# Sliding-window attention and token-mixing MLP on one core: k and q loaded in other pieces, the mask on VectorE, the last stores on two queues, and a new order of all work

## Chip, cores and metric

The kernel runs on one core of a Trainium2 chip. The metric is device time in microseconds, the median of repeated executions of the whole program. PE is TensorE, DVE VectorE, ACT ScalarE, POOL GpSimd and SP SyncE.

## What is computed

q, k and v are float32 of shape (8 batches, 8 heads, 576 tokens, 64). The attention has a window of 128 tokens back and a bias that falls with distance, with a slope of its own for each head; the second part mixes the tokens of each batch.

```python
rel = pos[:, None] - pos[None, :]
mask = (rel >= 0) & (rel < 128)
scores = where(mask, q @ k.T / 8 - slope[head] * abs(rel), -1e9)
x = softmax(scores) @ v                    # heads side by side: (8, 576, 512)
wq, wk = x @ w_q, x @ w_k                  # (8, 576, 64)
mixed = (wq @ wk.T / 8) @ x
out = relu(mixed) @ w_out                  # float32 (8, 576, 512)
```

## The kernel before, in words

All work is cut into some 690 named operations. `add(...)` declares each with its dependences; the text `ORDER` (lines 45 to 113) lists all of them by name with the engine that does each (P PE with the bank of PSUM, A ACT, D DVE, G POOL, S SP), and `follow` (line 140) emits them in that sequence. Every engine works through its own part of the list in order, so an operation that waits holds those behind it on its engine. A name ends in the batch and, behind the point, the part: QK4.2.0 is batch 4, key block 2, first half of the heads.

For each batch the stages are these:

- **Loads** (`Lq`, `Lk`, `Lv`, `Lt`; lines 374 to 394, issued by POOL, which converts float32 to float16). q of a batch is one load (`dma_q`) in which partition p holds rows 4p to 4p+3 of each head, so a run of 256 elements is contiguous in memory. k comes in four loads of 128 rows (`dma_k`, 64 elements to a run), v in five, and the last 64 rows of q and k of a pair of batches in `Lt`. For batch 0 six float32 loads, `LF`, are issued by SP and ACT instead, and reach the transposes `TF` and their copies `EF` without conversion. There are three buffers for k (`NNAT`), two for q (`NQ`), four for v.
- **Transposes** (`TQ`, `TK`, for batch 0 `TF` and `TJ`, tails `TT`) on PE with an identity matrix as second operand, each followed by a copy out of PSUM into `qkT` (`ETQ`, `ETK`, `EJ`, `ETT`). `TQ` (line 531) has 32 transposes of 128x64 that write column halves of PSUM, 128 columns each. `TK` (line 549) has sixteen in row halves (`tp2`, line 240): the upper and lower 64 partitions of two heads at once, 64 columns each. Both copies write dense rows.
- **Attention**: `QK` makes the scores of a key block for four heads in a pair of banks, `EXP` (ACT, line 639) exponentiates 128x1024 of them, `MUL` (DVE, line 654) multiplies both halves with a table `bias` of exp(-slope x distance), which is zero outside the window, `PV` (line 681) multiplies with v, and `RC` and `X` (DVE, lines 705 and 715) divide by the sums.
- **Mixing**, for pairs of batches: `XT`, `WK`, `WQ`, `WT`, `G`, `MX` on PE with their copies `EXT`, `EWK`, `EWQ`, `EWT`, `EG`, `RM`; then `OUT` (four matmuls of 512 columns), its copy `EO`, and the store `DO` (lines 932 to 970), all on SP. The last row group, `LAST` = (7, 3), is done in two halves, a and b.

Ahead of this stand the constants. POOL makes the identity (`ident`) and distances (`iota`, lines 303 to 305); DVE converts these (`wmc`, line 324); POOL puts a large number outside the window with four selects (`mask`, line 307); ACT makes the eight tables (`bias`, line 340). `WM` are matmuls on zeros that fill gaps of PE near the start; `WARM` gives the number in each group, 21 in all.

In the order of before POOL begins with Lq0.2, Lk0.2, Lk0.1, then ident and iota, and mask after Lk1.0. PE begins so:

```python
WM.0 TF0.1.0 TF0.1.1 WM.1 TJ0.2.0 TF0.0.0 TJ0.2.1 TF0.0.1 WM.2 QK0.2.1 TJ0.1.1 WM.3 QK0.2.0
```

Of the kernel before, what the change touches and what calls it, by code (L numbers as in the profile page):

```python
# [45 lines left out]
warm:D LF0.0.1.0:A LF0.0.1.1:A LF0.1.0.1:S pads:D Lq0.2:G LF0.1.0.0:S ones.0:D LF0.0.0.0:S
Lk0.2:G LF0.0.0.1:S Lk0.1:G ident:G iota:G Lq1.0:G wmc:D ones.2:D WM.0:P31 TF0.1.0:P00 Lk1.0:G
idh:D TF0.1.1:P01 EF0.1.0:D mask:G EF0.1.1:D WM.1:P31 TJ0.2.0:P00 Lk0.3:G bias:A TF0.0.0:P01
Lk1.1:G EJ0.2.0:D TJ0.2.1:P1 zeros:D TF0.0.1:P20 Lt0:G ones.3:D EJ0.2.1:D WM.2:P21 QK0.2.1:P1
TJ0.1.1:P3 EF0.0.0:A Lv0.1:G EJ0.1.1:D EXP0.2.1:A ones.1:D WM.3:P21 QK0.2.0:P0 Lv0.0:G  # L50
EF0.0.1:D EXP0.2.0:A WM.4:P31 QK0.0.1:P2 Lk1.3:G QK0.1.0:P1 QK0.1.1:P3 EXP0.0.1:A MUL0.2:D
TQ1:P0 Lv0.2:G EXP0.1.0:A Lk1.2:G QK0.0.0:P2 ETQ1:D EXP0.0.0:A Lv0.3:G TK1.0:P1 TJ0.3.1:P0
EXP0.1.1:A Lv0.4:G ETK1.0:D MUL0.0:D EJ0.3.1:A WM.5:P21 QK1.1.1:P1 QK1.0.0:P3 QK1.0.1:P2
EXP1.1.1:A TT0:P0 Lq2.0:G ETT0:D EXP1.0.1:A ETT1:D QK0.3.1:P1 Lv1.1:G MUL0.1:D EXP0.3.1:A
PV0.0:P0 Lk2.1:G QK0.3.0:P2 RC0.0:D X0.0:D EXP0.3.0:A PV0.1:P1 Lk2.0:G QK1.1.0:P0 RC0.1:D
EXP1.0.0:A Lv1.0:G PV0.2:P2 X0.1:D MUL0.3:D EXP1.1.0:A XT0.0:P10 Lv1.3:G TK1.1:P3 EXT0.0:A
Lv1.2:G MUL1.1:D PV0.4:P11 PV0.3:P0 Lv1.4:G ETK1.1:A RC0.2:D X0.2:D WM.6:P10 QK1.2.0:P3 RC0.3:D
QK1.2.1:P2 X0.3:D EXP1.2.0:A MUL1.0:D WM.7:P10 TQ2:P0 Lk2.2:G EXP1.2.1:A Lk2.3:G QK1.3.1:P3
RC0.4:D ETQ2:D QK1.3.0:P2 EXP1.3.1:A XT0.1:P10 Lw1:G MUL1.2:D EXP1.3.0:A TK2.0:P0 Lt1:G
PV1.1:P3 EXT0.1:A X0.4:D ETK2.0:D PV1.0:P2 Lv2.1:G RC1.0:D QK2.0.1:P0 X1.0:D QK2.0.0:P1  # L60
EXP2.0.1:A Lw0:G MUL1.3:D PV1.2:P2 Lk3.1:G EXP2.0.0:A RC1.2:D PV1.3:P0 X1.2:D Lk3.0:G PV1.4:P10
RC1.3:D RC1.1:D TK2.1:P2 X1.3:D Lq3.0:G ETK2.1:A X1.1:D QK2.1.1:P0 Lv2.0:G XT1.1:P11 RC1.4:D
EXP2.1.1:A QK2.1.0:P2 EXT1.1:D Lk3.3:G XT1.0:P30 EXP2.1.0:A X1.4:D QK2.2.1:P0 EXT1.0:D Lk3.2:G
TT2:P1 EXP2.2.1:A ETT3:D WK0:P30 Lv2.2:G MUL2.1:D Lv2.4:G QK2.2.0:P0 EWK0:A XTT0:P2 WQ0:P31
EXTT0:D EXP2.2.0:A Lv2.3:G ETT2:D MUL2.0:D WT0:P30 Lq4.0:G EWQ0:A QK2.3.1:P0 EWT0:A TK3.0:P1
MUL2.2:D QK2.3.0:P2 EXP2.3.1:A G0:P30 Lwo1:G EXP2.3.0:A ETK3.0:D TQ3:P0 Lwo0:G EG0:D MX0.0:P3
Lk4.1:G ETQ3:D PV2.1:P2 RM0.0:A MX0.3:P1 Lk4.0:G RC2.1:D MX0.1:P0 RM0.3:A X2.1:D QK3.0.1:P3
Lv3.0:G MUL2.3:D PV2.0:P2 RM0.1:A TK3.1:P1 Lq5.0:G RC2.0:D EXP3.0.1:A ETK3.1:D PV2.2:P0 Lv3.2:G
X2.0:D MX0.4:P1 QK3.2.1:P3 RMT0:A RC2.2:D PV2.3:P2 X2.2:D EXP3.2.1:A MX0.2:P1 RC2.3:D
QK3.0.0:P0 X2.3:D Lv3.4:G RM0.2:A TQ4:P3 EXP3.0.0:A QK3.3.1:P1 ETQ4:D Lv3.3:G XT2.0:P20  # L70
EXP3.3.1:A QK3.1.1:P0 PV2.4:P21 EXT2.0:D QK3.2.0:P3 EXP3.1.1:A Lv3.1:G RC2.4:D OUT1.3:P10
X2.4:D MUL3.0:D EXP3.2.0:A Lk4.3:G XT2.1:P11 QK3.3.0:P0 EO1.3:A Lk4.2:G TK4.0:P2 QK3.1.0:P3
EXP3.3.0:A ETK4.0:D OUT0.1:P10 Lk5.0:G EXT2.1:D EXP3.1.0:A PV3.0:P2 MUL3.3:D OUT0.0:P00 EO0.1:A
QK4.0.1:P3 EO0.0:A RC3.0:D QK4.0.0:P1 X3.0:D OUT0.2:P01 EXP4.0.1:A Lk5.1:G MUL3.2:D QK4.1.0:P2
EXP4.0.0:A Lk6.0:G TQ5:P3 MUL3.1:D EXP4.1.0:A Lt2:G PV3.4:P00 PV3.3:P1 RC3.4:D ETQ5:A X3.4:D
PV3.1:P2 RC3.3:D X3.3:D OUT1.4:P00 Lv4.3:G RC3.1:D X3.1:D QK4.1.1:P1 Lk7.1:G EO1.4:A TK4.1:P3
EO0.2:D PV3.2:P2 EXP4.1.1:A Lv5.1:G ETK4.1:D OUT1.1:P00 RC3.2:D Lk6.1:G X3.2:D TK5.0:P3 EO1.1:A
QK4.2.1:P1 ETK5.0:D Lv4.0:G XT3.0:P01 EXP4.2.1:A XTT2:P2 QK5.0.1:P3 Lv4.1:G EXTT2:D XT3.1:P00
EXP5.0.1:A EXT3.0:D QK5.1.0:P2 Lv4.2:G QK4.2.0:P1 EXT3.1:D EXP5.1.0:A WT2:P01 MUL4.0:D Lk5.2:G
TT4:P3 EXP4.2.0:A WK2:P00 Lv5.4:G ETT4:D EWT2:A ETT5:D QK4.3.0:P1 Lk5.3:G MUL4.2:D QK5.0.0:P2  # L80
EXP4.3.0:A WQ2:P01 Lv5.0:G MUL4.1:D EWK2:A QK5.1.1:P3 TK6.0:P1 Lq6.0:G EXP5.0.0:A G2:P00 EWQ2:D
Lk7.0:G EXP5.1.1:A ETK6.0:D QK4.3.1:P2 Lk6.3:G OUT1.2:P01 MUL5.0:D EXP4.3.1:A Lk6.2:G PV4.0:P3
EG2:A PV4.2:P1 RC4.0:D EO1.2:A Lv4.4:G X4.0:D MX2.4:P2 RMT2:A MX2.0:P0 RC4.2:D Lv5.3:G TK5.1:P3
X4.2:D RM2.0:A MX2.3:P2 ETK5.1:D Lt3:G OUT0.3:P10 RM2.3:A MUL5.1:D PV4.1:P3 EO0.3:A QK5.2.1:P2
RC4.1:D Lk7.2:G PV5.1:P0 X4.1:D EXP5.2.1:A MX2.2:P1 RC5.1:D MX2.1:P3 MUL4.3:D RM2.2:A Lq7.0:G
TQ6:P2 Lv6.3:G X5.1:D RM2.1:A XT4.0:P10 ETQ6:D PV4.3:P0 Lv5.2:G EXT4.0:A QK5.2.0:P3 OUT2.3:P11
Lv7.1:G RC4.3:D EXP5.2.0:A X4.3:D Lk7.3:G PV4.4:P10 EO2.3:A QK5.3.1:P0 RC4.4:D TK6.1:P3 X4.4:D
Lv6.0:G EXP5.3.1:A QK5.3.0:P2 ETK6.1:D XT4.1:P11 OUT1.0:P10 MUL5.2:D EXP5.3.0:A Lv6.2:G
QK6.1.0:P0 EO1.0:A TK7.0:P3 EXT4.1:D Lv6.1:G TT6:P2 EXP6.1.0:A OUT3.1:P10 ETK7.0:D ETT7:D
PV5.0:P3 ETT6:D EO3.1:A QK6.2.1:P0 RC5.0:D QK6.0.1:P2 X5.0:D EXP6.2.1:A OUT2.1:P10 Lv7.0:G  # L90
MUL5.3:D EXP6.0.1:A XT5.0:P11 Lv6.4:G QK6.0.0:P0 EO2.1:D QK6.3.0:P3 EXP6.0.0:A PV5.2:P2 Lv7.4:G
EXT5.0:D DO2.1:S OUT3.0:P10 RC5.2:D EXP6.3.0:A DO0.1:S Lv7.3:G X5.2:D DO1.3:S PV5.3:P0 EO3.0:A
# [62 lines left out]
def kernel(  # L155
# [151 lines left out]
    def mk_mask(o):  # L307
        def keep(c0, pattern, base, sign):
            n = 1
            for _, m in pattern:  # L310
# [2 lines left out]
            nc.gpsimd.affine_select(out=w, in_=w, compare_op=ALU.is_ge, fill=1.0e9, base=base,
                                    pattern=[[sign * st, m] for st, m in pattern], channel_multiplier=-sign)
# [729 lines left out]
```

## Time and profile before

| | us |
|---|---|
| median of 3 timed runs | 140.65 (140.08 to 140.69) |
| profiled execution | 139.65 |
| its span, first to last instruction | 137.9 |
| busy: PE, DVE, ACT, POOL | 124.5, 108.9, 109.9, 79.4 |
| mean granted clock of PE | 0.988 |

The profile is that of one execution. The span is shorter than the time of the execution by what lies before the first and after the last instruction. A busy PE is not a PE at its peak, since matmuls are pipelined and their ends are modelled. Durations of a form of instruction are means over its whole group; the distance between two in a row is shorter than that, because an instruction starts while the one before it still drains.

### The profile page before, as it was taken

Reading aid. Unit: us, or ns where it says so; the run is one execution under the profiler, and the core shown is the slowest. Engines: PE = TensorE matmul, PEld = TensorE weight load, DVE = VectorE, ACT = ScalarE, POOL = GpSimd, SP = SyncE. Lnnn points to the kernel's source line nnn. Section 1 sums busy time; section 2 is a strip of 40 time slices with the busy share of each in tenths; the row PEclk is TensorE's granted clock in tenths of the full one; section 3 lists DMA queues with packets and bytes.
Section 4 is the critical chain, followed back from the end, with each engine's and each line's share of the span. In section 5 each row is a group of like instructions: output and inputs, shape, how many; then the busy total and the mean of one; then the engine's idle time right before and its main releaser. Section 6 shows DMA issues by size and latency. Waiting matters only on the chain.

```text
span 137.9 us, 5054 instructions
## 1 busy us (share of the span) xinstructions
PE 124.5 (90%) x2173; PEld 80.3 (58%) x2173; DVE 108.9 (79%) x191; ACT 109.9 (80%) x149; POOL 79.4 (58%) x103
## 2 busy tenths in 40 slices
PE   6979777896899899999999999999999999999960
PEld 2353546584677576476756677676776685634430
DVE  3443789999899979999999999989999998084230
ACT  0376999898798999998999999999999890758430
POOL 6998989599989748699999599740000000000000
PEclk9977999999999999999999999999999999999999
...
GB/s 98 185 175 170 155 156 182 160 154 155 147 171 160 200 183 182 160 153 157 155 156 183 160 157 184 155 180 273 363 107 0 255 338 27 184 269 149 374 362 114
DMA packets 96055, 24.98 MB, mean 181 GB/s; under 512 B 83104, under 2 KB 91552, under 8 KB 96032
## 3 DMA queue, kind: packets, MB, share of 16 engines
...
q14 instruction: 6, 0.05, 0.1%
...
## 4 chain that ended last, share of the span: by engine, by line
PE 65%; DVE 15%; ACT 7%; DMA 7%; issue 2%; DVEq 0%; ACTq 0%; POOLq 0%
PE pair L235 52%; PE pair L238 13%; ACT pt L639 6%; DMA natq<-in_q_dram 5%; DVE pt L654 5%; DVE x L715 4%; DVE qkT L249 3%; DMA out_dram<-osb 2%; DVE inv L705 1%; DVE xT L249 1%; DVE xtl L709 0%; ACT qkT L247 0%; DVEq L1039 0%; ACT osb L247 0%; ACT rmt L860 0%
## 5 line engine op out<-in xcount | busy, mean ns | idle before, releaser
L639 ACT ACTIVATE pt<-pair 128x1024 f16<-128x1024 f32 x64 | 62.2, 1039 | 3.5 <-PE pair L235 3.1
L654 DVE TENSOR_TENSOR pt<-pt,bias 128x2048 f16<-128x2048 f16 x32 | 38.5, 1214 | 0.2 <-ACT pt L639 0.2
L393 POOL DMA_DIRECT2D vt<-in_v_dram x40 | 34.2, 874 | 3.8 <-DMA natq<-in_q_dram 1.8
L235 PE MATMUL pair<-wout_sb,rm 128*128 128x512 f16 (+1 forms) x132 | 31.2, 373 | 0.1
L375 POOL DMA_DIRECT2D natk<-in_k_dram x31 | 27.7, 909 | 5.4 <-DMA natq<-in_q_dram 2.8
L247 ACT COPY osb<-pair 128x512 f32<-128x512 f32 x30 | 17.8, 596 | 9.7 <-PE pair L235 8.6
L235 PE MATMUL pair<-qkT 64*128 64x256 f16 (+2 forms) x320 | 22.7, 250 | 2.5 <-DVE qkT L249 1.7
L249 DVE COPY qkT<-pair 128x1024 f16<-128x1024 f16 (+2 forms) x29 | 20.0, 704 | 6.3 <-PE pair L238 6.2
L235 PE MATMUL pair<-vt,pt 128*128 128x65 f16 (+1 forms) x576 | 21.7, 194 | 1.9 <-ACT pt L639 0.5
L235 PEld LDWEIGHTS <-pt 128*128 128x128 f16 (+1 forms) x576 | 19.0, 100 | 7.3 <-issue 3.0
L715 DVE TENSOR_TENSOR x<-pair,inv 128x512 f16<-128x512 f32 x32 | 21.9, 690 | 0.8
L235 PEld LDWEIGHTS <-rm 128*128 128x128 f16 x132 | 11.5, 98 | 12.3 <-issue 1.9
L235 PEld LDWEIGHTS <-qkT 64*128 64x128 f16 x320 | 10.8, 94 | 10.8 <-issue 5.1
L860 ACT ACTIVATE rm<-pair 128x1024 f16<-128x1024 f32 x12 | 11.7, 1023 | 1.4 <-PE pair L235 1.2
L238 PE MATMUL pair<-identh,x 128*128 128x128 f16 x128 | 9.9, 220 | 0.2 <-DVE x L715 0.2
L238 PE MATMUL pair<-identh,natq 128*64 128x128 f16 (+1 forms) x256 | 8.3, 217 | 1.6 <-DMA natq<-in_q_dram 1.3
L235 PE MATMUL pair<-warm 128*128 128x512 f16 x21 | 8.5, 526 | 1.2 <-DVE warm L290 1.2
L238 PEld LDWEIGHTS <-natq 128*64 128x64 f16 (+1 forms) x256 | 7.5, 110 | 3.1 <-DMA natq<-in_q_dram 1.8
L249 DVE COPY osb<-pair 128x512 f32<-128x512 f32 (+1 forms) x7 | 4.2, 610 | 6.4 <-PE pair L235 4.4
L238 PEld LDWEIGHTS <-x 128*128 128x128 f16 x128 | 7.6, 98 | 2.7 <-issue 1.3
L379 POOL DMA_DIRECT2D natq<-in_q_dram x8 | 7.3, 911 | 1.9 <-POOLq L1028 0.8
L249 DVE COPY xT<-pair 128x1024 f16<-128x1024 f16 x12 | 8.1, 683 | 0.3 <-PE pair L238 0.3
...
## 6 DMA issues: line engine op xcount, KB each, us to landing
out_dram<-osb SPq DMA_DIRECT2D x31, 256.0 KB, 3.0
...
```

Of the source, the lines that this page charges most:

```text
L235: hold(nc.tensor.matmul(*a, **k))
L238: hold(nc.tensor.transpose(*a))
L247: hold(nc.scalar.copy(out_ap, in_ap))
L249: hold(nc.vector.tensor_copy(out=out_ap, in_=in_ap))
L375: return lambda: nc.gpsimd.dma_start(out=natk(b, n), in_=k[b, :, P * n:P * n + P, :].transpose([1, 0, 2]))
L379: return lambda: nc.gpsimd.dma_start(out=natq_s[b % NQ][r0 // QR:P].rearrange("p h r d -> p h (r d)"), in_=q[b, :, r0:512, :].rearrange("h ...
L393: return lambda: nc.gpsimd.dma_start(out=vtv(b, t)[:n, :, 0:D], in_=v[b, :, P * t:P * t + n, :].transpose([1, 0, 2]))
L639: nc.scalar.activation(out=pt, in_=two(hold_.bank).rearrange("p e c -> p (e c)"), func=AF.Exp, scale=SCALE)
L654: nc.vector.tensor_tensor(out=pv, in0=pv, in1=bt, op=ALU.mult)
L705: nc.vector.reciprocal(out=box["inv"], in_=sums(p)[:, :, :, 64])
L715: nc.vector.tensor_tensor(out=x_s[b % NX][qt].rearrange("p (g h d) -> p g h d", g=2, h=4), in0=sums(p)[:, :, :, 0:64], in1=box["inv"].unsq ...
L860: hold(nc.scalar.activation(out=out_ap, in_=in_ap, func=AF.Relu, scale=WSCALE))
```

## The change

- k of batches 1 to 3 (`EARLYK`) is one load each, in the layout of q (partition p holds rows 4p to 4p+3). The three buffers for k become one tile each. `TK` of these batches has sixteen transposes of 128x64 with 128 columns each, for half of the heads and all keys; its copy `ETK` puts the columns back into order of keys, so that it writes every fourth element.
- q of batches 5 to 7 (from `LATEQ`) is four loads, one for each r of the rows 4p+r, with 64 elements to a run. `TQ` of these has 32 transposes in row halves over pairs of heads, 64 columns each.
- `mask` goes from POOL; `wmc` on DVE is three passes instead of one, which put a number of at least 1e7 where the distance is below 0 or above 127.
- The stores of the rows 0 to 511 of batch 7 may be issued by ACT; the order does so for DO7.2 and DO7.3b.
- `WARM` has 9, 3, 2 and 5 matmuls, 19 in all.
- The order is new as a whole: sequence, engines and banks. The engine of some copies changes with it: ETK goes from 2 on ACT and 12 on DVE to 6 and 8, EO from 30 and 7 to 27 and 10, ETT from 0 and 8 to 2 and 6; ETQ2 goes to ACT, ETQ5 to DVE.

The new order, its first part (to the last exponential of batch 3 and a little past it) and its end:

```diff
+WARM = (9, 3, 2, 5,)
+warm:D LF0.0.1.1:A LF0.0.0.0:S LF0.0.1.0:A ones.3:D ident:G LF0.1.0.1:S iota:G LF0.1.0.0:S
+Lk0.1:G wmc:D LF0.0.0.1:S Lq0.2:G idh:D bias:A Lk0.2:G ones.0:D zeros:D Lq1.0:G ones.1:D
+WM.0:P31 TF0.1.1:P00 Lk1.0:G TF0.0.0:P01 Lv0.0:G EF0.0.0:A Lk0.3:G WM.1:P31 TJ0.1.1:P1 Lt0:G
+TF0.1.0:P01 EJ0.1.1:D EF0.1.0:D ones.2:D WM.2:P31 QK0.0.0:P1 TF0.0.1:P01 EXP0.0.0:A Lv0.1:G
+TJ0.2.0:P20 EF0.0.1:D Lv0.2:G EF0.1.1:A TJ0.2.1:P3 EJ0.2.0:D EJ0.2.1:A QK0.0.1:P0 Lv1.0:G
+EXP0.0.1:A QK0.2.1:P3 QK0.2.0:P2 QK0.1.0:P1 EXP0.2.1:A MUL0.0:D QK0.1.1:P0 EXP0.1.0:A Lq2.0:G
+TQ1:P3 EXP0.2.0:A ETQ1:D EXP0.1.1:A MUL0.2:D WM.3:P11 TK1.0:P30 Lv0.3:G TK1.1:P31 ETK1.0:A
+PV0.0:P0 Lv1.1:G ETK1.1:D QK1.0.0:P2 TJ0.3.1:P1 Lk2.0:G EXP1.0.0:A RC0.0:D EJ0.3.1:D QK1.0.1:P3
+X0.0:D QK1.1.1:P1 EXP1.0.1:A QK1.2.0:P2 MUL0.1:D QK1.1.0:P0 Lv0.4:G EXP1.1.1:A TT0:P3 MUL1.0:D
+Lv1.2:G EXP1.1.0:A PV0.1:P1 ETT1:D Lv1.3:G ETT0:D EXP1.2.0:A MUL1.1:D QK0.3.1:P3 Lv1.4:G
+PV0.2:P0 EXP0.3.1:A QK0.3.0:P2 RC0.1:D RC0.2:D X0.1:D EXP0.3.0:A QK1.3.0:P3 X0.2:D PV1.0:P1
+EXP1.3.0:A MUL0.3:D QK1.3.1:P2 TQ2:P0 Lt1:G EXP1.3.1:A pads:D PV0.3:P3 RC1.0:D ETQ2:A PV1.1:P2
...
+ETK3.1:A Lv3.4:G MUL2.3:D QK3.1.1:P1 EG0:A Lk5.0:G PV2.0:P3 EXP3.1.1:A QK3.0.0:P2 RC2.0:D
+Lq5.03:G PV2.1:P0 X2.0:D EXP3.0.0:A MX0.1:P1 RC2.1:D MX0.3:P3 X2.1:D RM0.1:A Lk5.1:G MX0.0:P2
+RM0.3:D PV2.2:P0 RM0.0:A QK3.0.1:P1 RC2.2:D PV2.3:P3 X2.2:D EXP3.0.1:A QK3.2.0:P2 RC2.3:D
+QK3.2.1:P0 X2.3:D Lv3.3:G EXP3.2.0:A TQ4:P1 MUL3.0:D Lv3.2:G EXP3.2.1:A PV2.4:P30 MX0.2:P2
+ETQ4:D XT2.1:P31 RM0.2:A QK3.3.0:P0 Lq5.01:G RC2.4:D QK3.3.1:P1 X2.4:D EXP3.3.0:A OUT1.3:P20
+EXT2.1:D Lq5.00:G EXP3.3.1:A MUL3.2:D QK3.1.0:P0 Lq5.02:G TK4.0:P3 OUT0.1:P21 EXP3.1.0:A
+ETK4.0:D Lv3.1:G OUT0.2:P10 MUL3.3:D EO1.3:A Lk4.3:G EO0.1:A QK4.0.0:P0 TK5.0:P3 EO0.2:D
...
+OUT6.2:P01 DO7.0:S EO6.1:A OUT7.1:P20 DO6.1:S EO6.2:A OUT7.3b:P00 DO6.2:S EO7.1:A OUT7.3a:P01
+EO7.3b:A DO7.1:S EO7.3a:D DO7.3b:A DO7.3a:S
```

The functions, with the lines that only carry names along left out:

```diff
+    def rows_k(b):
+        return natk_s[b % NNAT].rearrange("p n h d -> p (n h d)").rearrange("p (h r d) -> p h r d", h=H, r=QR)
...
     def mk_wm(o):
-        nc.vector.tensor_copy(out=wm, in_=wint)
+        nc.vector.tensor_scalar(out=wm, in0=wint, scalar1=-127.0, scalar2=0.0, op0=ALU.add, op1=ALU.max)
+        nc.vector.scalar_tensor_tensor(out=wm, in0=wint, scalar=-1.0, in1=wm, op0=ALU.mult, op1=ALU.max)
+        nc.vector.scalar_tensor_tensor(out=wm, in0=wm, scalar=1.0e7, in1=wint, op0=ALU.mult, op1=ALU.add)
...
+    def dma_ka(b):
+        return lambda: nc.gpsimd.dma_start(
+            out=rows_k(b).rearrange("p h r d -> p h (r d)"),
+            in_=k[b, :, 0:512, :].rearrange("h (p r) d -> p h (r d)", r=QR))
...
+    def dma_qr(b, r):
+        return lambda: nc.gpsimd.dma_start(
+            out=rows_q(b)[:, r],
+            in_=q[b, :, 0:512, :].rearrange("h (p r) d -> r p h d", r=QR)[r])
...
+                        if late:
+                            x = rows_q(b)[:, r, 2 * c:2 * c + 2, :].rearrange("p a b -> p (a b)")
                         for e in range(2):
+                            if late:
+                                k = slice(64 * e, 64 * e + 64)
+                                dst = twoh(o.bank)[:, e].rearrange(
+                                    "p (c t r x) -> p c r t x", c=NHP, t=2, r=QR)[:, c, r]
+                                tp(dst, x[k], identh[k, k])
...
+            def emk(o):
+                for c in range(2):
+                    for r in range(QR):
+                        for e in range(2):
+                            o0 = 512 * c + P * r
+                            tp(oneh(o.bank)[64 * e:64 * e + 64, o0:o0 + P],
+                               rows_k(b)[:, 2 * (2 * u + c) + e, r, :], identh)
...
+            def evk(o):
+                cp(o.eng, qkT_s[b % 2][:, 1, 2 * u:2 * u + 2, 0:512].rearrange("p c (x r) -> p c r x", r=QR),
+                   oneh(tk.bank).rearrange("p (c r x) -> p c r x", c=2, r=QR))
...
+            store = nc.scalar if o.eng == "ACT" else nc.sync
```

More of the change, by code (lines that the diff above doesn't have):

```diff
@@ L41 @@
 LAST = (7, 3)
-WARM = (9, 2, 3, 1, 2, 1, 2, 1,)
+EARLYK = (1,2,3,)
+LATEQ = 5
+WARM = (9, 3, 2, 5,)
 ORDER = """
[L46 to L92, printed above, removed]
@@ new lines @@
+TQ5:P0 EXP4.1.1:A EXTT2:D QK4.1.0:P2 ETQ5:D Lq7.00:G PV3.2:P3 EXP4.1.0:A WT2:P10 Lv4.4:G
+RC3.2:D QK4.0.1:P0 EWT2:A X3.2:D QK5.1.1:P2 Lv4.0:G OUT0.0:P11 EXP5.1.1:A MUL4.1:D Lv4.1:G
+PV3.0:P3 EO0.0:A XT3.1:P10 RC3.0:D Lv4.2:G PV3.1:P2 X3.0:D EXP4.0.1:A OUT1.4:P11 RC3.1:D
+Lk5.2:G EXT3.1:A X3.1:D XT2.0:P00 MUL4.0:D Lv5.0:G EO1.4:A QK5.0.0:P2 TK4.1:P3 EXP5.0.0:A
+Lk5.3:G QK5.1.0:P1 ETK4.1:D XT3.0:P01 EXP5.1.0:A EXT2.0:D Lk6.0:G QK5.0.1:P2 QK4.2.1:P3
+EXT3.0:D OUT0.3:P00 EXP4.2.1:A Lq6.02:G MUL5.1:D TT4:P1 Lv4.3:G EXP5.0.1:A QK4.2.0:P3 WK2:P01
@@ L184 @@
     natq_s = [cpool.tile([P, H, QR, D], F16, name=f"natq{i}") for i in range(NQ)]
-    natk_s = [[cpool.tile([P, H, D], F16, name=f"natk{i}{n}") for n in range(4)] for i in range(NNAT)]
+    natk_s = [cpool.tile([P, 4, H, D], F16, name=f"natk{i}") for i in range(NNAT)]
     natt_s = [cpool.tile([P, 2, H, D], F16, name=f"natt{i}") for i in range(2)]
@@ L360 @@
     iota = add("iota", "", "", -59.5, {"POOL": (0.33, 0.33)}, [], mk_iota)
-    wmc = add("wmc", "", "", -59.4, DVE(0.35), [iota], mk_wm)
-    mask = add("mask", "", "", -39.985, {"POOL": (0.9, 0.9)}, [wmc], mk_mask)
-    mkb = add("bias", "", "", -30, ACT(2.6), [mask], mk_bias)
-    dst_ = not LOGB or add("dist", "", "", -30, DVE(0.6), [mask], mk_dist)
+    wmc = add("wmc", "", "", -59.4, DVE(1.2), [iota], mk_wm)
+    mkb = add("bias", "", "", -30, ACT(2.6), [wmc], mk_bias)
+    dst_ = not LOGB or add("dist", "", "", -30, DVE(0.6), [wmc], mk_dist)
     isc = not LOGB or add("idsc", "", "", -29, DVE(0.9), [idh], mk_idsc)
@@ L422, in lk @@
                 first32(1, n)
+            elif b in EARLYK:
+                if n == 0:
+                    x = load(("Lk", b, n), next(i), [dma_ka(b)], 1, [t for m in range(4) for t in tq.get((b - NNAT, m, 1), [])])
+                    for m in range(4):
+                        loads[b, 1, m] = x
             else:
@@ L428, in lq @@
                 first32(0, n)
+            elif b >= LATEQ:
+                loads[b, 0, n] = [load(("Lq", b, f"{n}{r}"), next(i), [dma_qr(b, r)], 1, tq.get((b - NQ, 2, 0), []))
+                                  for r in range(QR)]
             else:
@@ L531, in add_tq @@
         if n == 0:
+            late = b >= LATEQ
             def em(o):
@@ L934, in dm @@
             def dm(o, cs=cs, box=box):
[L935 to L937 removed]
+                (nc.scalar if o.eng == "ACT" else nc.sync).dma_start(
+                    out=rows_of(b, st)[:, cs], in_=box["o"][:, 0:256])
+            add("DO", b, f"{st}{'ab'[h]}", want + 1.8, {"SP": (0.7, 2.5), "ACT": (0.7, 2.5)}, [e], dm)
     def add_out(b, st, want):
```

111 lines of the change are left out of this document (68 added, 43 removed).

## The prediction

> **What bounds the kernel now.** I read the busy times by stage first, then the chain of work that ended last, then the waits and each engine's work in order of time. The first rows give the stretch, its length, the busy time of PE, of PE's weight loads, of DVE, ACT and POOL, then the granted clock.
>
> ```profile
> 6.90:8.60 1.70, 0.72 (x33) 0.69 (x34) 0.00 (x0) 0.94 (x3) 1.70 (x6) 1.00 1.96 164
> 8.60:10.30 1.70, 1.70 (x14) 1.13 (x15) 1.51 (x4) 1.70 (x5) 1.70 (x3) 0.57 1.72 186
> 13.70:15.40 1.70, 1.15 (x20) 0.68 (x20) 1.48 (x3) 1.40 (x2) 1.70 (x3) 1.00 2.43 155
> 20.00:50.00 30.00, 25.81 (x591) 19.49 (x591) 28.71 (x51) 26.50 (x33) 26.03 (x32) 1.00 2.02 168
> 50.00:100.00 50.00, 49.55 (x975) 33.08 (x972) 46.79 (x77) 48.44 (x62) 35.86 (x42) 1.00 2.11 186
> 125.00:130.00 5.00, 5.00 (x25) 2.27 (x24) 1.29 (x2) 2.98 (x6) 0.00 (x0) 1.00 0.69 228
> ```
>
> There are three stages. To about 14 us the kernel waits for its first data. From 20 to 50 us DVE (28.7 of 30 us) and ACT (26.5) are the tight engines, and PE has 4.2 us of gaps. From 50 us to its last matmul PE is the bound (49.55 of 50), but ACT and DVE are nearly full beside it: to 100 us they have gaps of 1.6 and 3.2 us. So a saving on one engine cannot be large; it must be spread, or come from the two ends. The next rows are in order of time: start, length, engine, what.
>
> ```profile
> 1.25 0.81 POOL L379 DMA_DIRECT2D natq<-in_q_dram  x1 [0.80 <-POOLq L1028]
> ...
> 3.80 0.23 POOL masks.py:197 MEMSET ident<- 128x128 f32 x1
> 4.11 0.29 POOL masks.py:199 TENSOR_SCALAR_AFFINE_SELECT ident<-ident 128x128 f32<-128x128 f32 x1
> 4.36 0.36 POOL L304 IOTA wint<- 128x256 int32 x1
> 4.67 0.23 POOL L305 IOTA wint<- 128x128 int32 x1
> ...
> 6.66 0.96 POOL L313 TENSOR_SCALAR_AFFINE_SELECT wm<-wm 128x128 f32<-128x128 f32 x4
> ```
>
> ```profile
> 0.74 1.10 ACTq L412 DMA_DIRECT2D osb<-in_k_dram  x2
> ...
> 4.94 0.36 DVE L325 CAST wm<-wint 128x384 f32<-128x384 int32 x1 [2.46 <-POOL wint L305]
> ...
> 5.38 1.28 ACT L343 ACT_TABLE_LOAD   x1 [5.38 <-DVE wm L325]
> 7.66 3.42 ACT L343 ACTIVATE bias<-wm 128x384 f16<-128x384 f32 x8 [1.00 <-POOL wm L313]
> ...
> 12.66 1.94 ACT L639 ACTIVATE pt<-pair 128x1024 f16<-128x1024 f32 x2 [1.11 <-PE pair L235]
> ...
> 55.13 2.02 ACT L639 ACTIVATE pt<-pair 128x1024 f16<-128x1024 f32 x2
> ```
>
> The first exponential starts at 12.66 us; the last of batch 3 (EXP3.1.0) ends at 57.15 us. The list of ACT's waits from 12 to 60 us (time, times, longest) has:
>
> ```profile
> ACT pt L639 <- PE pair L235: 2.7, 5, 1.1
> ACT qkT L247 <- PE pair L238: 1.0, 1, 1.0
> ACT rm L860 <- PE pair L235: 0.6, 1, 0.6
> ACT wk L247 <- PE pair L235: 0.3, 1, 0.3
> ```
>
> That is 4.6 us; less the 1.11 ahead of the first exponential, 3.5 us between the two.
>
> **The change part by part.** Single durations come from the groups by shape (busy, mean ns of one):
>
> ```profile
> L249 DVE COPY qkT<-pair 128x1024 f16<-128x1024 f16 x13 | 8.8, 680 | 2.3 <-PE pair L238 2.3
> L249 DVE COPY qkT<-pair 128x2048 f16<-128x2048 f16 x6 | 7.3, 1222 | 1.6 <-PE pair L238 1.6
> L862 DVE TENSOR_SCALAR rm<-pair 128x1024 f16<-128x1024 f32 x4 | 4.8, 1222 | 0.7 <-PE pair L235 0.5
> L247 ACT COPY qkT<-pair 128x1024 f16<-128x1024 f16 x2 | 2.2, 1084 | 1.0 <-PE pair L238 1.0
> L247 ACT COPY qkT<-pair 128x2048 f16<-128x2048 f16 x1 | 1.9, 1897 | 0.0
> L247 ACT COPY osb<-pair 128x512 f32<-128x512 f32 x30 | 17.8, 596 | 9.7 <-PE pair L235 8.6 <-issue 1.0
> L375 POOL DMA_DIRECT2D natk<-in_k_dram x31 | 27.7, 909 | 5.4 <-DMA natq<-in_q_dram 2.8 <-PE pair L235 1.3 <-DMA natk<-in_k_dram 0.6
> ```
>
> *Head.* POOL now makes the identity and the iota first: 0.23 + 0.29 + 0.36 + 0.23 = 1.1 us from 1.25, so to 2.35 us. The mask goes (0.96 on POOL; it held bias back by 1.00); in its place DVE makes three passes over 128x384. One took 0.36. The two new ones have no row; I bound each by 0.36 and by 1.22 (L862, over 1024 elements) and take 0.5, nearer to the row of the same size: wm stands at 2.35 + 1.4 = 3.8, in a time in which DVE waited for the iota (2.46 us). Table load 1.28 and bias 3.42 then end at 8.5 instead of 11.08 us, and EF0.0.0 behind them (0.6) at 9.1. The other condition is data. PE's new order puts TJ0.1.1, which needs the first k load of POOL (Lk0.1, issued at 2.35), ahead of TF0.1.0 and QK0.0.0. The k loads landed 5.1 to 9.7 us after their issue, and the load that stands first on POOL now took 6.6 (KB, us):
>
> ```profile
> DMA to landing us min/median/max: 5.1/7.3/9.7
> ...
> natq<-in_q_dram POOLq DMA_DIRECT2D x1, 256.0 KB, 6.6
> ```
>
> I take 6.6: landed at 8.95 us. Then TJ0.1.1, TF0.1.0 and QK0.0.0 (0.3 each, an estimate from the short PE pieces below) with a copy of 0.6 between them, 1.5 us: first exponential at 10.5, **-2.2 us**. With 5.1, ACT decides (9.5, -3.2); with 9.7 it is 13.6 (+0.9).
>
> *k of batches 1 to 3.* Nine POOL issues go (0.91 us each), so these loads are issued up to 8 us earlier. After 20 us neither PE nor its weight loads waited on a DMA, so this helps batch 1 only. The price: each of six TK turns from sixteen row-half transposes into sixteen of 128 columns. The chain has both kinds back to back, and eight of XT (start, length, what):
>
> ```profile
> 41.70 0.23 PE pair L238 x16
> ...
> 54.25 0.45 PE pair L238 x8
> ...
> 59.40 1.01 PE pair L238 x32
> ```
>
> Half of 1.01 against 0.23: +0.27 x 6 = 1.6 us of PE before 45 us, inside PE's 4.2 us of gaps; at most 1.6 if those close. The six copies now write every fourth column. No row shows such a f16 write: on DVE I bound it by 0.68 and 1.22 and take 1.2 (L862, which also reorders its elements); on ACT by 1.08 and 1.90, and take 1.08, the row of its size. Five of the six go to ACT (before, two), and the order hands ACT more. From the first exponential to EXP3.1.0, at 0.6 for 512 elements and 1.08 for 1024, ACT gains EF0.1.1, EJ0.2.1, ETT2, EG0 (2.4), five ETK (5.4) and ETQ2 (1.9), in all 9.7; it loses EJ0.3.1, EWQ0, EWT0, RMT0, EO1.3 (3.0), two ETK, EXT0.1 and one RM (4.3), in all 7.3: **+2.4 us**, while DVE has some 1 us less. So ACT becomes the bound of this stage. Of its 3.5 us of waits I let half go (K of batch 1 is there earlier, and the wait of 1.0 stood ahead of a TK copy that changes place): **-1.8**, bounds 0 and -3.5. EXP3.1.0 would end near 55.6. But there the new order still owes PE XT2.0, TK4.0 and MX0.4 (0.45 + 0.23 + about 0.2): **+0.9**.
>
> *q of batches 5 to 7.* TQ5 to TQ7 become 32 row-half transposes of 64 columns: 2 x 0.23 = 0.46 against 1.01, so -0.55 x 3 = -1.65 us of PE where PE is the bound; bounds 0 (as many instructions as before) and -1.65. The copies keep a dense inner run (1.22 on DVE; ETQ5 leaves ACT, -1.9 there). DVE and ACT must follow, and their gaps of 3.2 and 1.6 us would nearly close, so I count two thirds: **-1.1**. Nine more POOL issues (8 us) come here, where POOL was busy 35.86 of 50 us, after nine fewer ahead of them:
>
> ```profile
> 90.49 0.88 POOL L393 DMA_DIRECT2D vt<-in_v_dram  x1 [0.19 <-PE pair L235]
> ```
>
> So the last load stays near 90 us, lands by about 98 and is used after 110; that cover of over 10 us hides it, and I cost it at nothing; if it came 8 us later it would still be hidden. A quarter that waits for its buffer (TQ3, TQ4, TQ5) holds the v and k loads behind it on POOL, as one load did before: at nothing, at most 1 us.
>
> *Tail.* The last matmul ends at 133.30; then DVE makes both half copies, and SP issues both stores:
>
> ```profile
> 124.48 8.82 PE L235 MATMUL pair<-wout_sb,rm 128*128 128x512 f16 x44
> 133.39 0.75 DVE L249 COPY osb<-pair 128x256 f32<-128x256 f32 x2 [1.96 <-DMA out_dram<-osb]
> 133.84 0.84 SPq L935 DMA_DIRECT2D out_dram<-osb  x2
> ```
>
> With 7.3b copied and issued by ACT, only one half copy and one issue follow the last matmul: half of 0.75, **-0.4** (bounds 0 and -0.84). DO7.2 on ACT (half of the 1.10 for two issues there) lies in ACT's gaps: ACT was busy 2.98 of the 5 us before 130.
>
> *Sum.* -2.2 + 2.4 - 1.8 + 0.9 - 1.1 - 0.4 = **-2.2 us**. The profiled execution took 139.65 us with a span of 137.9; it lies 1.0 under the median of the timed runs, 140.65, and the difference goes on the median: **138.4 us**.
>
> **The rivals.**
>
> *More comes through.* ACT runs without waits and PE keeps all its saving: -2.2 + 2.4 - 3.5 + 0.9 - 1.65 - 0.4 = -4.45, so 136.2. For it: after 60 us PE waited on nothing but one copy, for 0.2 us. Against: ACT would be full for 45 us on end. 0.15.
>
> *The PE saving is given back.* ACT and DVE, 97 and 94% busy from 50 us, set the pace: without the -1.1 it is 139.5. 0.15.
>
> *The clock.* After a stretch with PE busy 0.72 of 1.70 us (6.9 to 8.6) the granted clock fell to 0.57. The new order has two warm matmuls fewer, a wait for Lk0.1 of up to 2 us, and then mostly transposes. If the low clock lasted to 18 us, TQ1, the five matmuls of WM.3 (0.2 each, as 44 of that width took 8.82) and both TK1, 3.0 us together, would take twice that ahead of QK1.0.0; about 0.8 of it lies beside the copy of TQ1. That is +2.2 on the forecast: 140.6. The Trainium skill, "TensorE: Matmul & The Clock Gate", Part 4, says that transposes do not count as busy for the clock gate in the same way, which speaks for this rival and against the change. The trace bears it out only in part: from 13.7 us the clock is 1.00, though most of PE's work there is transposes. 0.10.
>
> *ACT gives the head back and more (slower).* From 10 to 55 us ACT is the bound with 2.4 us more work. If its old waits all come back (each engine waits for a bank that another must empty), with Lk0.1 landing after 7.5 us and PE's saving lost on a late ACT: -1.3 + 2.4 + 0.9 - 0.4 = +1.6, so 142.2. It decides where less than 0.9 us of the 2.9 that I count for waits and for TQ comes through. For it: three engines near full leave an order little room. 0.18.
>
> *The change does not do what it says.* Row halves save nothing, or the strided copy costs 1.9 on ACT (5 x 0.82 more): 139.5 to 142.5. 0.05.
>
> **How the numbers follow.** The forecast has 0.37 (its own range 137.2 to 139.3). A measurement of this kernel can tell about 0.5%, 0.7 us, from no change, so same is 139.95 to 141.35. Faster holds the forecast, the first two rivals and a little of the last: 0.69, and the clock rival, which straddles that bound, 0.10 of same. Slower: 0.18 and the rest of the last, 0.21. The range reaches from 135.6, a little under the case in which more comes through, to 142.2, the slower rival; the worst bounds of the head and of the strided copy are left out above.
>
> **What would show it.** First exponential near 10.5 us and no later than 11.4; bias done by 9 us; clock 1.00 from 14 us on. ACT close to 30 of 30 us from 20 to 50 us, and DVE below 28.7. EXP3.1.0 ends near 55.6. The strided copies take 1.08 on ACT and 1.2 on DVE, TQ5 to TQ7 0.46 in the chain. PE is full from 60 us on, and from its last matmul to the end of the span it is 0.4 us less. I am wrong if the first exponential starts after 12 us, if the copies cost 1.9, or if PE has over 1 us of gaps after 60 us.

## The result, and the profile after

The changed kernel is slower: 146.12 us (144.33 to 147.39, 4 runs) against 140.37 us for the kernel before on the same chip (139.43 to 140.69, 4 runs). The ratio is 1.038, with a 95% interval of 1.027 to 1.049. The prediction was 138.4 us, with a range of 135.6 to 142.2. The profiled execution took 146.03 us with a span of 144.3. The medians here are of all executions, but the ratios leave out those that ran over 1.5% longer than the fastest of their kernel, and where the profile of an experiment is that of such an execution (the strided read, the tail, the head alone), only durations of DVE, ACT and DMA work are read from it.

The head came out better than predicted. In the timeline of the changed kernel (start, length, engine, what; in brackets the idle time before and what ended it):

```profile
1.84 0.36 DVE L318 TENSOR_SCALAR wm<-wint 128x384 f32<-128x384 int32 x1
1.86 1.28 ACT L338 ACT_TABLE_LOAD   x1 [1.86 <-issue]
2.24 0.56 DVE L319 SCALAR_TENSOR_TENSOR wm<-wint,wm 128x384 f32<-128x384 int32 x1
2.83 0.56 DVE L320 SCALAR_TENSOR_TENSOR wm<-wm,wint 128x384 f32<-128x384 f32 x1
3.42 3.41 ACT L338 ACTIVATE bias<-wm 128x384 f16<-128x384 f32 x8 [0.28 <-DVE wm L320]
...
9.67 1.02 ACT L691 ACTIVATE pt<-pair 128x1024 f16<-128x1024 f32 x1 [2.36 <-PE pair L242]
```

bias ends at 6.83 us, and the first exponential starts at 9.67 instead of 12.66. So the loss lies behind it. The windows of the changed kernel (start and end, length, busy PE, PE's weight loads, DVE, ACT, POOL, the granted clock) show where:

```profile
17.00:20.00 3.00, 1.28 (x31) 0.94 (x28) 2.78 (x3) 2.38 (x1) 1.92 (x3) 0.90 2.40 156
20.00:22.00 2.00, 1.91 (x26) 1.29 (x21) 1.70 (x3) 1.91 (x3) 1.86 (x4) 0.50 1.55 195
...
20.00:50.00 30.00, 23.67 (x514) 17.91 (x508) 25.01 (x46) 29.37 (x26) 20.98 (x27) 0.90 1.80 172
50.00:60.00 10.00, 9.47 (x148) 6.18 (x149) 6.71 (x11) 8.36 (x10) 8.07 (x10) 0.66 2.42 156
```

From 20 to 50 us ACT is full, as predicted (29.37 of 30 us), but PE is busy 23.67 us where it was busy 25.81, though the change gives PE more work here. From 17 to 20 us ACT's 2.38 busy us are one instruction (x1). The clock is below 1 three times: in windows of 1 us it is between 0.50 and 0.74 from 19 to 23, from 36 to 40 and from 50 to 57 us. The timeline names the instruction:

```profile
16.95 2.43 ACT L254 COPY qkT<-pair 128x1024 f16<-128x1024 f16 x1 [0.44 <-PE pair L245]
...
17.40 2.42 DVE L256 COPY qkT<-pair 128x1024 f16<-128x1024 f16 x1
...
19.44 0.61 PE L242 MATMUL pair<-qkT 64*128 64x256 f16 x4 [1.72 <-ACT qkT L254]
```

These are the two copies ETK1.0 and ETK1.1, which write every fourth column: 2.43 us on ACT, 2.42 on DVE. QK1.0.0 needs the first of them (its four heads are in that half), and PE is idle for 1.72 us until it ends; it starts at 19.44, before the second copy ends at 19.82. Just behind this gap, from 20 to 22 us, the granted clock is 0.50. The other two stretches of low clock lie in the same way behind waits of PE for strided copies (1.23 and 0.86 us ahead of QK2.2.0 and QK2.1.1, 2.26 us ahead of QK3.1.1). The groups by shape (busy, mean ns of one) and PE's waits from 12 to 60 us (time, times, longest) say the same:

```profile
L254 ACT COPY qkT<-pair 128x1024 f16<-128x1024 f16 x6 | 13.2, 2254 | 1.1 <-ACT osb L254 0.7 <-PE pair L245 0.4
L256 DVE COPY qkT<-pair 128x1024 f16<-128x1024 f16 x9 | 7.9, 873 | 0.1
```

```profile
PE pair L242 <- ACT qkT L254: 6.4, 5, 2.3
PE pair L242 <- ACT pt L691: 0.7, 3, 0.3
```

Both groups are mixed. Of the six on ACT five are strided and one, ETK5.0, is dense (1.01 us): (6 x 2.254 - 1.01) / 5 = 2.5 us each. Of the nine on DVE one is strided. Then the end of batch 3:

```profile
60.27 2.90 ACT L691 ACTIVATE pt<-pair 128x1024 f16<-128x1024 f32 x3
```

EXP3.1.0 ends at 63.17 us instead of 57.15: 6.0 us later, with a head 3.0 us earlier. From there to the last matmul it is 76.6 us (139.78) against 76.15 before. So all of the loss, and 3 us more, arose between 10 and 63 us. The tail, in the timeline:

```profile
131.84 7.94 PE L242 MATMUL pair<-wout_sb,rm 128*128 128x512 f16 x40
...
139.84 0.36 ACTq L987 DMA_DIRECT2D out_dram<-osb  x1
139.88 0.42 DVE L256 COPY osb<-pair 128x256 f32<-128x256 f32 x1 [2.83 <-ACT osb L254]
140.33 0.33 SPq L987 DMA_DIRECT2D out_dram<-osb  x1
```

The last matmul ends at 139.78, the span at 144.3: 4.5 us, against 4.6 before.

### The profile page after: what moved, and what is told of

The parts are those of the page before. It is cut to its first block, busy times and chain, and to the rows that moved or that the text cites. A ratio compares the mean times of both kernels' runs of the same rounds, so it can differ in the third digit from the quotient of the medians.

```text
span 144.3 us, 5019 instructions
## 1 busy us (share of the span) xinstructions
PE 127.1 (88%) x2171; PEld 81.5 (56%) x2171; DVE 112.0 (78%) x193; ACT 119.9 (83%) x149; POOL 78.3 (54%) x99
## 4 chain that ended last, share of the span: by engine, by line
PE 52%; DVE 21%; ACT 16%; DMA 4%; issue 3%; POOL 1%; DVEq 0%; POOLq 0%; ACTq 0%
PE pair L242 43%; ACT qkT L254 9%; PE pair L245 9%; ACT pt L691 7%; DVE pt L706 7%; DVE qkT L256 6%; DVE x L767 5%; DMA natk<-in_k_dram 4%; DVE xT L256 1%; DVE inv L757 1%; DVE osb L256 1%; ACT xT L254 0%; POOL wint L311 0%; POOL ident masks.py:199 0%; DVE xTt L256 0%
## 5 line engine op out<-in xcount | busy, mean ns | idle before, releaser
L242 PE MATMUL pair<-qkT 64*128 64x256 f16 (+2 forms) x320 | 25.3, 268 | 8.2 <-ACT qkT L254 6.4
L242 PE MATMUL pair<-vt,pt 128*128 128x65 f16 (+1 forms) x576 | 23.7, 200 | 0.8 <-ACT pt L691 0.3
L256 DVE COPY qkT<-pair 128x1024 f16<-128x1024 f16 (+2 forms) x23 | 18.3, 805 | 4.2 <-PE pair L245 4.0
L254 ACT COPY osb<-pair 128x512 f32<-128x512 f32 (+1 forms) x27 | 15.5, 585 | 7.3 <-PE pair L242 7.3
L369 POOL DMA_DIRECT2D natk<-in_k_dram x19 | 17.7, 965 | 1.3 <-PE pair L242 1.1
L254 ACT COPY qkT<-pair 128x1024 f16<-128x1024 f16 (+2 forms) x10 | 16.8, 1716 | 1.5 <-PE pair L245 0.8
L386 POOL DMA_DIRECT2D natq<-in_q_dram x12 | 11.3, 965 | 11.5 <-PE pair L245 11.5
L757 DVE RECIPROCAL inv<-pair 128x8 f32<-128x8 f32 x32 | 6.2, 199 | 6.5 <-PE pair L242 5.5
L256 DVE COPY osb<-pair 128x512 f32<-128x512 f32 (+1 forms) x10 | 6.6, 662 | 5.6 <-ACT osb L254 3.7
L245 PE MATMUL pair<-identh,natk 64*128 64x64 f16 (+1 forms) x248 | 7.8, 203 | 1.0 <-DMA natk<-in_k_dram 0.8
(71 smaller groups left out, 138.4 us busy)
```

The costliest lines, as they stand in the source:

```text
L242: hold(nc.tensor.matmul(*a, **k))
L245: hold(nc.tensor.transpose(*a))
L254: hold(nc.scalar.copy(out_ap, in_ap))
L256: hold(nc.vector.tensor_copy(out=out_ap, in_=in_ap))
L369: return lambda: nc.gpsimd.dma_start(out=natk(b, n), in_=k[b, :, P * n:P * n + P, :].transpose([1, 0, 2]))
L386: return lambda: nc.gpsimd.dma_start(out=rows_q(b)[:, r], in_=q[b, :, 0:512, :].rearrange("h (p r) d -> r p h d", r=QR)[r])
```

## Experiments

Three theories stood at the start. **Copies**: the strided write of ETK costs 2.4 us, ACT is full, and all behind it is late. **Order**: three engines near full leave the new order no room, whatever the copies cost. **Clock**: the low clock behind PE's gaps is what costs. The ratios below are to the kernel before on the same chip, with their 95% intervals.

### Dense write

```diff
-  cp(..., qkT_s[...].rearrange("p c (x r) -> p c r x", r=QR), ...
+  cp(..., qkT_s[...].rearrange("p c (r x) -> p c r x", r=QR), ...
```

Keys of batches 1 to 3 thereby stand in another order than the rest expects; the instructions are the same.

> The changed kernel, but the copies of k of batches 1 to 3 write their columns in the order in which they come, dense (keys of these batches then stand in another order, so scores and mask of these batches are not those of the reference). Theory 1, the strided write is the cause: a copy falls from about 2.45 to 1.08 us on ACT and from 2.42 to 0.68 on DVE, PE's waits for them go, the granted clock returns to 0.98 or more, and the time falls to 137.5 to 140. Theory 2, the new order with its load on ACT is the cause and the copies only add to it: five times 1.4 us go on ACT but waits come back elsewhere, 142.5 or more.

137.1 us, ratio 0.988 (0.980 to 0.996): 5.0 percentage points below the changed kernel's ratio. In the windows, waits and timeline of this kernel:

```profile
20.00:50.00 30.00, 26.82 (x621) 20.42 (x621) 28.74 (x55) 29.31 (x33) 20.75 (x26) 1.00 1.85 175
...
50.00:100.00 50.00, 49.56 (x1006) 32.90 (x1006) 48.67 (x80) 48.31 (x67) 41.72 (x49) 1.00 2.26 175
```

```profile
PE pair L242 <- ACT qkT L254: 0.3, 1, 0.3
```

```profile
51.01 2.85 ACT L691 ACTIVATE pt<-pair 128x1024 f16<-128x1024 f32 x3
```

PE's wait of 6.4 us for ACT's copies is 0.3, the clock is 1.00 from 4 to 120 us, and EXP3.1.0 ends at 53.86 instead of 63.17. The order is the same, so the theory of the order falls: it has room enough when a copy costs 1.0 us on ACT.

### Strided read

```diff
-  qkT_s[...].rearrange("p c (x r) -> p c r x", r=QR), oneh(tk.bank).rearrange("p (c r x) -> p c r x", c=2, r=QR)
+  qkT_s[...].rearrange("p c (x r) -> p c x r", r=QR), oneh(tk.bank).rearrange("p (c r x) -> p c x r", c=2, r=QR)
```

The copy now walks the keys in order: it reads PSUM with a step of 128 columns and writes dense. It computes what the reference does.

> The changed kernel, but the same copies run over keys in order: dense write, and the read from PSUM steps by 128 columns (4 reads apart, then the next). Theory 1a, only the write side is dear: 1.1 to 1.25 us a copy, time as with the dense copy (137.5 to 140.5). Theory 1b, any reordering costs: 2.4 us a copy, 145 to 147.

137.62 us, ratio 0.987 (0.980 to 0.995). In the timeline of this kernel, ETK1.0 and ETK1.1:

```profile
17.58 1.01 ACT L254 COPY qkT<-pair 128x1024 f16<-128x1024 f16 x1 [0.44 <-PE pair L245]
18.03 1.22 DVE L256 COPY qkT<-pair 128x1024 f16<-128x1024 f16 x1
```

The same elements in the same final places cost ACT as much as a dense copy when the step is on the side of the read, and DVE 1.22 instead of 0.68. This version is faster than both kernels, and than the one before by 1.3% (0.5 to 2.0).

### Every second column

```diff
-  "p c (x r) -> p c r x", r=QR  ...  c=2, r=QR
+  "p c (x r) -> p c r x", r=2   ...  c=2, r=2
```

The keys stand in a wrong order here too.

> The changed kernel, with the write of these copies at every second column in place of every fourth (keys in another order, so these batches are not the reference's). If the price is that of any step but one, a copy takes 2.4 us and the time stays near 146. If it grows with the distance, about 1.7 us and near 142.

138.2 us in one run, lower than either case expected. In its timeline:

```profile
17.35 1.30 ACT L254 COPY qkT<-pair 128x1024 f16<-128x1024 f16 x1 [0.44 <-PE pair L245]
17.80 1.30 DVE L256 COPY qkT<-pair 128x1024 f16<-128x1024 f16 x1
```

1.30 us on both engines: between dense (1.01 and 0.68) and every fourth column (2.43 and 2.42). So it isn't one price for any step: of the three steps tried, one, two and four columns, a wider one cost more, and on ACT two columns cost far less than the 1.7 us that was expected.

### Warm matmuls, three runs around the clock

The strided write kept, with 26 more matmuls on zeros in the three gaps of PE:

```diff
-WARM = (9, 3, 2, 5,)
+WARM = (9, 3, 2, 5, 8, 8, 10,)
-PV0.0:P0 Lv1.1:G ETK1.1:D QK1.0.0:P2
+PV0.0:P0 Lv1.1:G WM.4:P10 ETK1.1:D QK1.0.0:P2
...
+WM.5:P30 QK2.2.0:P0
...
+WM.6:P20 QK3.1.1:P1
```

> The changed kernel with its strided copies, and 26 more warm matmuls in the three longest gaps of PE (before QK1.0.0, QK2.2.0 and QK3.1.1). Clock theory: the stretches at half clock go (mean 0.98 or more) and the time falls to 142 or less. Strided-copy theory: clock up, but the ACT copies still set the pace to 50 us: 142.5 to 145.5.

143.74 us, ratio 1.033 (1.027 to 1.039), with the clock at 1.00 from 17 to 100 us and EXP3.1.0 at 60.13. This is the case that the strided-copy theory gave. The same 26 on the base of the strided read:

> The same base with the 26 further warm matmuls of the run that kept the strided writes. That run took about 0.5% off. If it did so by the clock alone, here, where the gaps that let the clock fall are gone, they can only cost: 0 to 2 us more than without them (ratio to before 0.987 to 1.002). If the order has a low clock of its own that the key copies did not cause, they save here too, 0.5 us or more (0.983 or below).

142.8 us, ratio 1.022 (1.017 to 1.026), so 3.4% more than without them, and above both cases of the expectation: where no copy makes PE wait, the 26 (26 x 0.2 us is 5.2 us) lie nearly in full on the path. PE as a whole is not full there (26.82 of 30 us from 20 to 50 in the dense version); but they stand ahead of the QK that ACT waits for. This spoils the first run as a test: what it gave back by the clock it partly took by its own work. Hence 10 (3, 3 and 4) with the strided write:

> The changed kernel with its strided writes, with 10 further warm matmuls (3, 3 and 4) in the three gaps of PE instead of 26. What is told apart: how much of the loss is the low clock behind those gaps. If the clock holds at 1.00 with so few, the time is that of the strided writes alone: EXP3.1.0 ends at 58 to 60 us instead of 63.2, and the ratio to before is 1.015 to 1.025. If 10 do not hold it, the ratio stays at 1.03 to 1.04 and the window from 50 to 60 us keeps a clock near 0.66. If the low clock is off the path, the clock rises and the time stays at 1.035 or above.

143.3 us, ratio 1.030 (1.024 to 1.036). Its windows:

```profile
20.00:50.00 30.00, 24.10 (x526) 17.66 (x524) 24.59 (x47) 29.87 (x28) 20.69 (x26) 1.00 1.83 173
50.00:60.00 10.00, 9.45 (x171) 6.27 (x172) 9.81 (x16) 10.00 (x13) 8.72 (x11) 1.00 2.43 156
```

Ten hold the clock at 1.00, and EXP3.1.0 ends at 59.63 instead of 63.17. The profiled executions thus put the low clock at 3.5 us of the delay, the ratios at 0.8% of the time (some 1.1 us, and with intervals that overlap). (The profiled executions are 3.6 us apart, 146.03 and 142.46 us, and the medians 2.8; but on the chip of the second the kernel before is 1.0 us faster too, 139.4 against 140.37.) The size stays open within these; the expectation (1.015 to 1.025) gave the clock too large a part. What is left, 1.030 against 0.988 with dense writes, is 4%. It is the copies, less what the ten matmuls cost by themselves; that is at most 10 x 0.2 = 2 us or 1.4%, and was not measured.

### q of batches 5 to 7 whole again

On the base of the strided read; Lq6 and Lq7 as Lq5, each whole load at the place of the first quarter:

```diff
-LATEQ = 5
+LATEQ = 8
-Lq5.03:G ... Lq5.01:G ... Lq5.00:G ... Lq5.02:G
+Lq5.0:G
```

> The changed order with the key copies writing densely (they read every fourth column of PSUM instead), and q of batches 5 to 7 again in one load each with 32 transposes of 128 rows, at the place of the first quarter in the order. What is told apart: whether the row-half transposes are worth time at the end. If PE sets the end and all that it saves comes through: TQ5 to TQ7 are 0.54 us longer each in the trace, the end 1.6 us later than with the row halves (ratio to before about 0.999 instead of 0.987). By the prediction, two thirds: 1.1 us later (0.995). If the saving is given back to ACT and DVE (rival): no later than with the row halves (0.987), and PE has 1.6 us fewer gaps after 60 us.

140.3 us in 12 runs, ratio 1.004 (1.001 to 1.007), so 1.6% or 2.3 us above the base. In its timeline TQ6 and TQ7 take 1.08 us again; the second fence has them as quarters, in the dense version, with 0.64 and 0.63 (the chain of waits counts 1.01 and 0.47):

```profile
81.08 1.08 PE L243 MATMUL pair<-identh,natq 128*64 128x128 f16 x32
88.91 1.08 PE L243 MATMUL pair<-identh,natq 128*64 128x128 f16 x32
```

```profile
78.76 0.64 PE L245 MATMUL pair<-identh,natq 64*128 64x64 f16 x32
...
86.00 0.63 PE L245 MATMUL pair<-identh,natq 64*128 64x64 f16 x32
```

So the row halves come through in full (1.65 us), and by the mean a little more. The further 0.6 us is within the intervals. It need not come from the transposes either, because the edit also moves loads: in its profile PE waits 0.58 us for a load of v and 0.16 for one of k, which it does not in the dense version. Without the row halves the rest of the change, with a dense write, gains nothing against before.

### Constants late

On the same base, identity and iota behind the first three loads on POOL:

```diff
-... ones.3:D ident:G LF0.1.0.1:S iota:G LF0.1.0.0:S
-Lk0.1:G wmc:D LF0.0.0.1:S Lq0.2:G idh:D bias:A Lk0.2:G ones.0:D
+... ones.3:D LF0.1.0.1:S LF0.1.0.0:S
+Lk0.1:G LF0.0.0.1:S Lq0.2:G Lk0.2:G ident:G iota:G wmc:D idh:D bias:A ones.0:D
```

> The same base (dense writes), with the identity and the iota made behind the first three loads on POOL instead of ahead of them: iota 2.6 us later, so bias ends near 9.5 instead of 6.8 us. What is told apart: whether an earlier first exponential moves the end. If the head counts one for one, as the sum took it: first exponential 1.5 to 2.5 us later, near 12, and the end as much later (ratio to before 0.998 to 1.005 instead of 0.987). If the middle gives it back (ACT's waits and PE's gaps absorb it): first exponential as late, but EXP3.1.0 and the end under 0.7 us later (0.987 to 0.992).

141.11 us, ratio 1.010 (1.005 to 1.015): 2.3% or 3.2 us above the base, a little more than expected, with the first exponential at 12.57. That is at least one for one. The clock from 12 to 20 us was 0.85 in its profile, so a part of the 3.2 us may be the clock's.

### The tail as before

```diff
-DO7.2:A  EO7.3b:A  DO7.3b:A
+DO7.2:S  EO7.3b:D  DO7.3b:S
```

> The same base, with both last half copies on DVE and all last stores on SP's queue, as before. Prediction's term: 0.4 us later than with two queues. By the trace of the changed kernel, whose stretch from last matmul to the end of the span is 4.5 us against 4.6: 0.1 us later, not to be told from nothing; then the store's own flight sets the end, not the issue.

138.53 us in 10 runs, ratio 0.989 (0.985 to 0.993) against 0.987: the two queues are worth nothing that can be told. The predicted 0.4 us would be 0.3%, less than these intervals resolve.

### Parts of the change in the old order

The order of before, k in quarters, with the early constants, the VectorE mask and the row halves (the four quarter loads of q together at the place of the whole one):

```diff
-Lq0.2:G LF0.1.0.0:S LF0.0.0.1:S ... ident:G iota:G ... mask:G
+ident:G iota:G Lq0.2:G LF0.1.0.0:S ...
-Lq5.0:G
+Lq5.00:G Lq5.01:G Lq5.02:G Lq5.03:G
```

> The order of before with k in quarters, as before, and of the change only two parts: the constants first (identity and iota at the head of POOL, mask on VectorE) and q of batches 5 to 7 by head pairs with row-half transposes. What is told apart: whether the gain of the dense version needs the new order. If the head counts one for one and the row halves 1.6 us or more: first exponential at 11 to 11.7 instead of 12.66 us (the first loads on POOL are issued 1.1 us later, so data now decides), TQ5 to TQ7 at 0.47 us, and a ratio to before of 0.975 to 0.985, below the dense version of the new order (0.987). If the new order is what lets the head and the row halves come through: 0.99 to 1.00.

141.59 us, ratio 1.015 (1.008 to 1.021): both expectations missed. The first exponential is at 11.38 us, as expected, but in the timeline of POOL and PE:

```profile
80.25 3.67 POOL L386 DMA_DIRECT2D natq<-in_q_dram  x4
83.72 2.81 POOL L400 DMA_DIRECT2D vt<-in_v_dram  x3
```

```profile
89.76 0.43 PE L242 MATMUL pair<-vt,pt 128*128 128x65 f16 x9 [1.14 <-DMA vt<-in_v_dram]
```

Four issues in a row (3.67 us) push the v loads back, and PE waits 1.14 us for one. The profiled execution took 139.74 us, though, where the median is 141.59 and the profiled execution of before took 139.65; so it does not show all of what is lost. With the quarters apart among the other loads:

> As the version with head and row halves in the old order (1.0147), but the four quarter loads of q stand apart among the v and k loads instead of together. There POOL's four issues in a row (3.5 us) ended in a wait of PE for a v load of 1.1 us. If that was the loss: the wait goes, PE keeps the row halves' 1.6 us and the ratio is 0.98 to 0.99. If nine further issues on a POOL that is full from 50 to 93 us are too many in this order, wherever they stand: PE still waits for a load and the ratio stays above 1.00.

145.44 us, ratio 1.045 (1.038 to 1.052), as the second case had it. The wait moved to q, twice:

```profile
61.68 0.55 PE L246 MATMUL pair<-identh,natq 64*128 64x64 f16 x26 [2.35 <-DMA natq<-in_q_dram]
84.03 0.55 PE L246 MATMUL pair<-identh,natq 64*128 64x64 f16 x26 [1.27 <-DMA natq<-in_q_dram]
```

These waits are 3.6 us, and behind the first of them, from 62 to 66 us, the granted clock is 0.65.

And the head alone, with q whole:

> The order of before with k and q as before, and of the change the constants-first head and the VectorE mask alone. What is told apart: whether the head is worth its time without the new order. The version with the row halves beside it had its first exponential at 11.38 instead of 12.66 us and EXP3.1.0 1.3 us earlier. One for one: 1.3 us earlier at the end, ratio to before 0.991. If the old order gives it back after 57 us: 0.997 to 1.003.

140.97 us in 12 runs, ratio 1.009 (1.004 to 1.014): slower, where 0.991 or no change was expected. In the old order PE starts on a load of POOL, which the constants delay by 0.5 us. In the chain of waits it is the first long piece, and PE's work on it follows. Before:

```profile
1.25 6.58 DMA natq<-in_q_dram
...
7.88 3.14 PE pair L238 x48
11.01 1.60 PE pair L235 x7
```

And in the version with head and row halves:

```profile
1.76 6.02 DMA natq<-in_q_dram
...
7.83 2.54 PE pair L245 x48
10.37 0.97 PE pair L242 x7
```

There it landed at 7.78 against 7.83 us. So the data came no later, but hardly earlier either. What brought the first exponential from 12.66 to 11.38 us is the same work of PE, 1.23 us shorter: the granted clock was 0.71 from 8 to 10 and 0.50 from 10 to 12 us before, and 1.00 in both here. That the first exponential came where it was expected was luck, then; the constants did not do it. In the profile of the head alone the load took 7.15 us and landed at 8.92, 1.1 us later than before. One execution does not explain the loss of 0.9%, and its cause stays open; but nothing here shows that the early constants by themselves bring the first exponential forward in the old order.

## Why the prediction was wrong

**The step that failed** is the price of the strided copy: "on ACT by 1.08 and 1.90, and take 1.08, the row of its size". It measured 2.43 to 2.62, above the upper bound, and on DVE 2.42 against bounds of 0.68 and 1.22. The lower bounds were rows of the same shape with a dense write; the upper ones were a dense row of twice the size (1.90) and one of another input type that writes runs of 32 elements (1.22). None writes with such a step, so none could hold its cost; "No row shows such a f16 write" was right, and what followed from it was not. Five copies at 1.4 us too little are 7 us on ACT, the engine that the same part called the bound of the stage. The case "the strided copy costs 1.9 on ACT" stood among the rivals with 0.05: the right mechanism, at 0.82 us extra where it is 1.4. The dense write and the strided read show it: 5.0% of the time goes with the step of the write alone, the low clock that its waits bring with them included. The slower rival, "ACT gives the head back and more", is not what happened, though it too forecast a slower kernel: with short copies the same order gives nothing back.

**The clock** was a rival, for another place. The low clock came behind PE's waits for the copies, not behind the wait for Lk0.1, and it went when the copies were short: in the changed kernel it is 1.00 in every window from 4 to 17 us, and in the dense version from 12 to 20 us too, though TQ1, both TK1 and TJ0.3.1 stand there (transposes are 2.45 of PE's 6.38 busy us). The prediction read its own row too strongly: from 13.7 to 20 us before, transposes are 72 of PE's 103 instructions but 2.2 of its 4.7 busy us, about half. What the prediction took from the Trainium skill, "TensorE: Matmul & The Clock Gate", Part 4, that transposes do not count as busy for the clock gate in the same way, isn't what decided here: the low clock came behind waits of PE, and went with them.

**Head.** Predicted -2.2, measured -3.0: POOL began at 0.74 instead of 1.25 us, the three passes of wm took 1.48 against 1.4, and Lk0.1 landed in 5.96 us against 6.6. The late constants show that it comes through to the end in this order. The term has no word for PE's clock: before, it was 0.71 and 0.50 from 8 to 12 us, and now 1.00. The row of the old order above, where the same work is 1.23 us shorter at full clock, suggests that some 1.2 of the 3.0 us is this.

**ACT's work and waits, PE's debt.** +2.4 - 1.8 + 0.9 put EXP3.1.0 at 55.6; the dense version, where the copies cost what was assumed, has 53.86 with a head that is 1.1 us better than assumed. These terms together hold within 1 us: from the first exponential to the end of EXP3.1.0 it is 44.45 us against 45.1 by the prediction (55.6 - 10.5), with 1.8 us more work and 1.8 us fewer waits on ACT than before. ACT full from 20 to 50 us was right as well.

**Row halves.** 0.47 against a predicted 0.46; two thirds was too cautious, all came through. DVE and ACT did not set the pace.

**POOL's buffers.** In the waits of the changed kernel:

```profile
POOL natq L386 <- PE pair L245: 11.5, 3, 7.8
```

Quarters waited 11.5 us for their buffers, once 7.8, and held the v and k loads; PE waited for no load after the head but 0.2 us. "At nothing" was right here, but by the lead that the loads have in this order, and in this kernel, whose middle is late; with the dense write the weight loads waited 0.4 us for v. In the old order the same issues made PE wait 1.14 us (together) or 3.6 us (apart).

**Tail.** -0.4 predicted, -0.1 measured, nothing shown by the experiment. The last issue did come earlier behind the last matmul (0.55 us against about 0.96, the second of the two in the prediction's row), but the end of the span lies 4.0 us after it instead of 3.6: what the shorter issue gave, the last store took.

**The sum** with the price of a dense copy was about right: 138.4 is 0.984 of 140.65, and the strided read gives 0.987 (0.980 to 0.995). Its single terms were less right than that: the head and the row halves gave 1.3 us more than counted and the tail 0.3 less, and the mean time shows nothing of the difference.
